# A seven-product scheme for the second matrix product of layer 2, with its weight factors made while layer 1 runs

## The chip, the cores and the metric

The kernel runs on one core of a Trainium2 chip. The metric is the device time of one execution, in microseconds (us). TensorE is called PE here, its weight loads PEld, VectorE DVE, ScalarE ACT, GpSimd POOL, and SyncE, which issues every DMA of this kernel, SP.

## What is computed

Attention in chunks of 64 tokens, then two feed-forward layers on 2304 tokens (width 512, inner width 2048):

```python
x   = chunked_attention(q, k, v)        # 4 x 8 heads x 576 x 64, as 2304 x 512
x2  = mish(x @ w_in1) @ w_out1          # layer 1
out = squareplus(x2 @ w_in2) @ w_out2   # layer 2; squareplus: h if h >= 1, 0 if h <= -1, else (h + 1)^2 / 4
```

The weights come as 64-bit floats, seen as pairs of 32-bit words, and are decoded to 32-bit floats on the chip.

## The kernel before, in words

**Numbers in two parts.** PE multiplies in a rounded 32-bit format (fp32r). To keep precision every operand a is split into hi = round(a) and lo = a - hi, and a product is three matmuls into one accumulator in PSUM: hi hi, hi lo, lo hi. So each operand costs a copy (hi; ACT or DVE) and a subtraction (lo; DVE or POOL), and is twice as large.

**Stages.** Tokens go in 6 blocks of 384 (NB) or 18 tiles of 128; the inner width in 16 row tiles j of 128 or 8 pairs jp.

1. Attention of all tokens, interleaved with the first product of layer 1 (`up`, L569, matmuls at L578): 6 blocks x 16 tiles x 12 matmuls of 384 columns. The activated results z go to DRAM (`z_store`). To about 278 us.
2. The second product of layer 1 (`down` with n = 0, matmuls at L630): per block and j 12 matmuls of 384 columns. `g_pair` (L594) loads a pair of z tiles, copies hi (L273 or L271) and subtracts lo (L608). From 278 us to about 474.
3. The first product of layer 2 (`seven`, L637, matmuls at L654). It uses Strassen's scheme in Winograd's form: a product of 2 x 2 blocks by seven block products in place of eight, at the price of additions. `x_seven` (L406) makes the seven token factors, `w_seven` (L387) the seven weight factors of a pair jp from the decoded weights. 24 units of 42 matmuls of 384 columns. DVE adds up the results (L672) and applies squareplus with ACT (L693, L696, L698). z goes to DRAM again. To about 661 us.
4. The second product of layer 2 (`down` with n = 1, also L630): per block and j, three token tiles by three matmuls of 512 columns, so 6 x 16 x 9 = 864. `g_pair` prepares z as in stage 2; at the end of a block three copies (L786) and three DMAs (L788) write the output. Its weights, split into hi and lo, were put into DRAM in stage 2 (L351) and are fetched by 16 DMAs at the end of stage 3 (`w_back`, L381).

**Weights.** `w_part(n, j)` (L282) decodes one tile of weight n (0 to 3: w_in1, w_out1, w_in2, w_out2): a load of 512 KB, a scaled copy on ACT (L301), a clamp on POOL (L304), three bit operations on DVE (L311, L318, L324), then for n = 2 a store (L344), for the others the split (L329, L333). Before, n = 2 and n = 3 are both decoded in stage 2: tile j of n = 2 is due at t2 + 5 j, of n = 3 at t2 + 82 + 5 j, where t1 is the start of stage 1 in the plan (33 us), t2 that of stage 2 and t3 that of stage 3.

**Order.** A planner (`Plan`, L27) lays every operation on its engine by lengths, due times and releases that stand in the code, and the program is emitted in this order. At run time each engine, and SP's queue, goes through its list strictly in that order.

**Memory.** 154 KB of each partition hold the split operands, at places set by hand (`PLACES`); the rest holds rings of buffers, "ld" (4 of 4 KB), "z2" (6 of 3 KB), "z" (2), "sh" (4) and "dec" (2). PSUM has two groups of four banks, A and B, used in turn.

Of the kernel before, what the change touches and what calls it, by code (L numbers as in the profile page):

```python
# [164 lines left out]
def kernel(  # L165
# [18 lines left out]

    nc = tc.nc
# [41 lines left out]
    for tag, n in PSUM.items():  # L227
# [54 lines left out]
    def w_part(n, j, tau, release=0.0, after=()):  # L282
# [5 lines left out]
        new(sh, "sh", [P, DM])  # L288
# [49 lines left out]
        op("ACT", 0.66, down, reads=[raw], writes=[dec], tiles=[raw, dec], **kw)  # L338
        op("POOL", 0.8, clamp, writes=[dec], tiles=[dec], **kw)
        op("DVE", 0.46, shift, reads=[dec], writes=[sh], tiles=[dec, sh], **kw)  # L340
        op("DVE", 0.69, sign, reads=[dec], writes=[sh], tiles=[dec, sh], **kw)
        op("DVE", 0.72, low, reads=[raw], writes=[sh], tiles=[raw, sh], **kw)
# [38 lines left out]
    def w_back(j, tau, after=()):  # L381
        w = ("wb", j)
        new(w, None, [P, 2, DM], F32R)
        dma(512, lambda _: nc.sync.dma_start(out=get(w).bitcast(F32).rearrange("p r d -> p (r d)"), in_=wd_split[j]),
            reads=[("wd", 3, j), *after], writes=[(w, 0), (w, 1)], tiles=[w], prio=tau)

    def w_seven(n, jp, tau):  # L387


        wf, sf, w = ("wf", n, jp), ("sf", n, jp), ("w7", n, jp)  # L390
        new(sf, "ld", [P, 4, 2 * P])
        new(w, None, [P, 7, 2, 2 * P], F32R)
        A = lambda f, d: lambda: get(wf)[:, f, d * 2 * P:(d + 1) * 2 * P]
# [3 lines left out]
        add(S(1), A(1, 0), A(1, 1), False, reads=[wf], writes=[K(1)], **kw)  # L397
        add(S(3), A(0, 0), A(1, 0), True, reads=[wf], writes=[K(3)], **kw)
        add(S(2), S(1), A(0, 0), True, reads=[wf, K(1)], writes=[K(2)], **kw)
        add(S(4), A(0, 1), S(2), True, reads=[wf, K(2)], writes=[K(4)], **kw)  # L400
        part = lambda a, b: lambda r: get(w)[:, a:b, r]
        split(part(0, 2), lambda: get(wf)[:, 0].rearrange("p (d f) -> p d f", d=2), 4 * P, (w, 0), tau, reads=[wf], tiles=[wf, w])
        split(part(2, 3), lambda: get(wf)[:, 1:2, 2 * P:], 2 * P, (w, 1), tau, reads=[wf], tiles=[wf, w])
        split(part(3, 7), lambda: get(sf), 8 * P, (w, 2), tau, reads=[K(i) for i in (1, 2, 3, 4)], tiles=[sf, w])

    def x_seven(q, tau, after=()):  # L406
# [3 lines left out]
        for d, t in ((0, 0), (0, 1), (1, 1), (1, 0)):  # L410
            x = xs[d, t] = ("xh", q, d, t)
            new(x, "ld", [P, 2, NB])
# [173 lines left out]
    def z_store(n, b, jp, tau):  # L586
        z = ("z", n, b, jp)
        dma(384, lambda _: nc.sync.dma_start(
            out=spill[n][b * NF // 2 + jp], in_=get(z).rearrange("p j t -> p (j t)")
        ), reads=[(z, 0), (z, 1)], writes=[("spill", n, b, jp)], tiles=[z], prio=tau)  # L590

    pairs = {}

    def g_pair(n, b, jp, tau):  # L594

        zl, g = ("zl", n, b, jp), ("g", n, b, jp)
        new(zl, ("z2", "ld")[n], [P, 2, NB])
# [14 lines left out]
    def down(n, b, j, tau):  # L612
        w, g, a = (("w", 1, j), ("wb", j))[n], ("g", n, b, j // 2), j % 2
        ys = [("y", n, b, m) for m in range((KD, TB)[n])]
        if j == 0:
            for y in ys:
                new(y, "AB"[b % 2], [P, 512])

        def products(_):
            wt, gt = get(w), get(g)  # L620
            for m, y in enumerate(ys):
                if n == 0:
                    wh, wl = (wt[:, x, m * P:(m + 1) * P] for x in range(2))
                    gh, gl = gt[:, 0, a], gt[:, 1, a]
                    o, prods = get(y)[:, 0:NB], ((wh, gh), (wh, gl), (wl, gh))
                else:
                    gh, gl = (gt[:, x, a, m * P:(m + 1) * P] for x in range(2))
                    o, prods = get(y), ((gh, wt[:, 0]), (gh, wt[:, 1]), (gl, wt[:, 0]))
                for x, (l, r) in enumerate(prods):
                    nc.tensor.matmul(  # L630
                        out=o, lhsT=l, rhs=r, start=(j == 0 and x == 0), stop=(j == NF - 1 and x == 2)
                    )

        op("PE", 2.09, products, reads=[(g, x) for x in range(2)] + [(w, 0), (w, 1)],
           writes=[*ys, ("step", n, b, j), *([("yend", n, b)] if j == NF - 1 else [])], tiles=[w, g, *ys], prio=tau)
# [100 lines left out]
    for b in range(NBLK):  # L736
        for j in range(NF):
            tau = due2(b, j)
            if j % 2 == 0:
                g_pair(0, b, j // 2, tau - 14)  # L740
            down(0, b, j, tau)
        for m in range(KD):
            y, yo = ("y", 0, b, m), ("yo", b, m)
            new(yo, "sh", [P, NB])
            op(("ACT", "DVE"), (0.49, 0.55), lambda e, yo=yo, y=y: copy(e, get(yo), get(y)[:, 0:NB]),
               reads=[("yend", 0, b)], writes=[yo], tiles=[yo, y], prio=tau)
            dma(192, lambda _, b=b, m=m, yo=yo: nc.sync.dma_start(out=x2d[b][:, m * NB:(m + 1) * NB], in_=get(yo)),
                reads=[yo], writes=[("x2d", b, m)], tiles=[yo], prio=tau)
    t3 = due2(NBLK, 0)
    for bp in range(NBLK // 2):  # L750
        x_seven(bp, (t2 + 80, t3 - 8, t3 + 8)[bp], after=[("step", 0, *((2, 0), (NBLK - 1, 10), (NBLK - 1, NF - 1))[bp])])
    for j in range(NF):
        w_part(2, j, t2 + 5.0 * j, release=t2 + 5.0 * j - 10)
    for j in range(NF):
        w_part(3, j, t2 + 82 + 5.0 * j, release=t2 + 72 + 5.0 * j)
# [8 lines left out]
    for u, (jp, bp) in enumerate(todo):  # L764
        if bp == 0:
# [3 lines left out]
                   after=[("hq", jp - 2, NQ - 1, 0) if jp > 1 else ("step", 0, NBLK - 1, 3 + 5 * jp)])  # L769
# [3 lines left out]
    due4 = lambda b, j: t4 + 2.06 * (b * NF + j)  # L773
    for b in range(NBLK):
        for j in range(NF):
            tau = due4(b, j)
# [6 lines left out]
        for m in range(TB):  # L783
            y, o = ("y", 1, b, m), ("o", b, m)
            new(o, "z", [P, DM])
            op(("ACT", "DVE"), (0.6, 0.69), lambda e, y=y, o=o: copy(e, get(o), get(y)),  # L786
               reads=[("yend", 1, b)], writes=[o], tiles=[y, o], prio=tau)
            dma(256, lambda _, b=b, m=m, o=o: nc.sync.dma_start(  # L788
                out=out[b * NB + m * P:b * NB + (m + 1) * P, :], in_=get(o)
            ), reads=[o], tiles=[o], prio=tau)  # L790
# [54 lines left out]
```

## Time and profile before

| | us |
|---|---|
| runs of the kernel before | 868.79, 868.91, 864.09 (median 868.79) |
| the profiled execution | 863.63 |
| its span, first to last instruction | 861.8 |
| PE busy in the span | 848.0 |
| DVE busy | 548.3 |
| ACT busy | 324.9 |
| POOL busy | 172.5 |

A group of instructions is named by line, engine, operation and shape; its figures are the time in which any of them ran, and the mean length of one in ns. PE's matmuls overlap, so the pace of a stream is not their mean length but the time of a run of them divided by their count. A row of the chain of waits has start, length and what ran. A table by stretch gives busy time and count for each engine, PE's granted clock (1.00 is 2.4 GHz) and the share of time in which the DMA engines moved data.

### The profile page before, as it was taken

What the parts mean: (1) busy time and instruction counts of PE and PEld (TensorE: products, weight loads), DVE (VectorE), ACT (ScalarE), POOL (GpSimd) and SP (SyncE); (2) the same over time, 40 slices, a digit from 0 to 9 for tenths busy, and PEclk for the clock granted to TensorE, in tenths of its full rate; (3) what the DMA queues carried; (4) which work ended last, traced back from release to release, by engine and by line L of the source; (5) the groups of instructions that cost most, each with busy time, mean ns of one, the idle gap of its engine ahead of it and who ended that gap; (6) DMA issues with size and microseconds to landing.
All of it is one profiled execution on the core that took longest, in us unless ns stands there. A gap on an engine that the chain in (4) does not pass through costs nothing.

```text
span 861.8 us, 14614 instructions
## 1 busy us (share of the span) xinstructions
PE 848.0 (98%) x5710; PEld 800.5 (93%) x5710; DVE 548.3 (64%) x875; ACT 324.9 (38%) x535; POOL 172.5 (20%) x154
## 2 busy tenths in 40 slices
PE   9999999999999999999999989999999999999997
PEld 8899999999999999999999989999999888888886
DVE  4998767575402677689888898777776343344331
ACT  3664646565422222224332366666655000000000
POOL 1474212110000201254443463111100000000000
PEclk9999999999999999999999999999999999999999
DMA  8779584867225779759986343333379443443431
GB/s 204 201 217 267 175 225 157 235 184 179 86 110 198 251 255 310 275 168 338 363 306 235 113 152 134 135 135 135 135 266 415 167 130 95 134 138 81 141 108 37
DMA packets 122149, 163.49 MB, mean 190 GB/s; under 512 B 62944, under 2 KB 82400, under 8 KB 122080
## 3 DMA queue, kind: packets, MB, share of 16 engines
q1 hardware_dynamic: 122080, 162.56, 58.5%
q8 instruction: 45, 0.74, 0.4%
q14 instruction: 24, 0.20, 0.1%
HBM read 102.76 MB, written 59.77 MB: 189 GB/s over the span
## 4 chain that ended last, share of the span: by engine, by line
PE 90%; DVE 6%; DMA 1%; issue 1%; ACT 1%; SPq 0%; POOL 0%; DVEq 0%; ACTq 0%; POOLq 0%
PE A L630 23%; PE B L578 21%; PE B L630 20%; PE B L654 10%; PE A L654 10%; PE B L812 2%; PE A L477 2%; PE A L493 1%; DVE memory L311 1%; PE A L549 1%; DVE memory L324 1%; DVE memory L318 1%; PE A L537 1%; DVE memory_r L608 1%; DVE memory_r L273 1%
## 5 line engine op out<-in xcount | busy, mean ns | idle before, releaser
L578 PE MATMUL B<-memory_r 128*128 128x384 f32 x1152 | 213.8, 339 | 1.0 <-POOL memory_r L333 0.8
L630 PE MATMUL B<-memory_r 128*128 128x384 f32 (+1 forms) x1008 | 203.5, 358 | 1.2 <-DVE memory_r L608 0.9
L630 PE MATMUL A<-memory_r 128*128 128x384 f32 (+1 forms) x1008 | 202.1, 358 | 0.4 <-DVE memory_r L608 0.4
L578 PEld LDWEIGHTS B<-memory_r 128*128 128x128 f32 x1152 | 197.6, 188 | 3.6 <-POOL memory_r L333 1.3
L630 PEld LDWEIGHTS B<-memory_r 128*128 128x128 f32 x1008 | 181.1, 188 | 18.8 <-DVE memory_r L608 1.4
L630 PEld LDWEIGHTS A<-memory_r 128*128 128x128 f32 x1008 | 181.1, 188 | 17.5 <-DVE memory_r L608 0.8
L273 DVE CAST memory_r<-memory 128x768 fp32r<-128x768 f32 (+2 forms) x109 | 64.7, 596 | 168.4 <-PE A L630 70.9
L608 DVE TENSOR_TENSOR memory_r<-memory,memory_r 128x768 fp32r<-128x768 f32 x96 | 101.7, 1060 | 18.6 <-ACT memory_r L271 11.3
L304 POOL TENSOR_SCALAR memory<-memory 128x512 f32<-128x512 f32 x64 | 53.3, 835 | 236.6 <-ACT memory L301 216.8
L271 ACT ACTIVATE memory_r<-memory 128x512 fp32r<-128x512 f32 (+3 forms) x80 | 58.4, 745 | 110.7 <-PE A L630 38.8
L654 PE MATMUL B<-memory_r 128*128 128x384 f32 x504 | 92.8, 337 | 3.4 <-DVE memory L672 3.4
L654 PE MATMUL A<-memory_r 128*128 128x384 f32 x504 | 93.2, 335 | 0.1
L654 PEld LDWEIGHTS B<-memory_r 128*128 128x128 f32 x504 | 88.5, 189 | 3.9 <-DVE memory L672 3.7
L654 PEld LDWEIGHTS A<-memory_r 128*128 128x128 f32 x504 | 88.3, 189 | 0.4 <-POOL memory_r L369 0.4
L727 ACT ACTIVATE memory<-B 128x384 f32<-128x384 f32 x96 | 46.0, 491 | 86.9 <-PE B L578 79.9
L271 ACT ACTIVATE memory<-A 128x512 f32<-128x512 f32 (+1 forms) x59 | 32.3, 559 | 114.4 <-PE A L630 64.8
L301 ACT ACTIVATE memory<-memory 128x512 f32<-128x512 f32 x64 | 42.7, 668 | 59.5 <-DMA memory<-in_moe_w_in_dram 34.3
L333 POOL TENSOR_TENSOR memory_r<-memory,memory_r 128x512 fp32r<-128x512 f32 x30 | 43.9, 1465 | 61.7 <-DVE memory_r L273 28.0
L318 DVE SCALAR_TENSOR_TENSOR memory<-memory 128x512 uint32<-128x512 uint32 x64 | 50.5, 793 | 1.2
L324 DVE SCALAR_TENSOR_TENSOR memory<-memory 128x512 uint32<-128x512 uint32 x64 | 49.9, 783 | 1.1
L271 ACT ACTIVATE memory<-B 128x384 f32<-128x384 f32 (+1 forms) x28 | 14.0, 505 | 94.6 <-PE B L630 80.0
L369 POOL TENSOR_TENSOR memory_r<-memory,memory_r 128x768 fp32r<-128x768 f32 (+3 forms) x21 | 40.3, 1923 | 36.7 <-ACT memory_r L271 24.0
(48 smaller groups left out, 644.2 us busy)
## 6 DMA issues: line engine op xcount, KB each, us to landing
z<-memory SPq DMA_DIRECT2D x96, 384.0 KB, 2.6
memory<-z SPq DMA_DIRECT2D x96, 384.0 KB, 4.3
memory<-in_moe_w_in_dram SPq DMA_DIRECT2D x32, 512.0 KB, 5.3
memory<-in_moe_w_out_dram SPq DMA_DIRECT2D x32, 512.0 KB, 5.0
v<-memory_r SPq DMA_DIRECT2D x16, 512.0 KB, 6.4
memory_r<-v SPq DMA_DIRECT2D x16, 512.0 KB, 8.8
memory<-in_v_dram SPq DMA_DIRECT2D x72, 64.0 KB, 3.6
x<-memory SPq DMA_DIRECT2D x24, 192.0 KB, 3.4
```

Of the source, the lines that this page charges most:

```text
L271: nc.scalar.activation(out=out, in_=in_, func=AF.Copy)
L273: nc.vector.tensor_copy(out, in_)
L301: nc.scalar.activation(out=get(dec), in_=get(raw)[:, :, 1].bitcast(F32), func=AF.Copy, scale=DOWN)
L304: nc.gpsimd.tensor_scalar(out=get(dec), in0=get(dec), scalar1=HIGH, scalar2=-HIGH, op0=ALU.min, op1=ALU.max)
L318: nc.vector.scalar_tensor_tensor(out=s, in0=d, scalar=0x80000000, in1=s, op0=ALU.bitwise_and, op1=ALU.bitwise_or)
L324: nc.vector.scalar_tensor_tensor(out=s, in0=get(raw)[:, :, 0], scalar=29, in1=s, op0=ALU.logical_shift_right, op1=ALU.bitwise_or)
L333: eng.tensor_tensor(out=get(w)[:, 1], in0=get(sh), in1=get(w)[:, 0].bitcast(F32), op=ALU.subtract)
L578: nc.tensor.matmul(out=ps, lhsT=a, rhs=xt[:, r, kk, :], start=(kk == 0 and y == 0), stop=(kk == KD - 1 and y == 2),)
L608: op("DVE", 0.98, lambda _: nc.vector.tensor_tensor(out=get(g)[:, 1], in0=get(zl), in1=get(g)[:, 0].bitcast(F32), op=ALU.subtract), reads= ...
L630: nc.tensor.matmul(out=o, lhsT=l, rhs=r, start=(j == 0 and x == 0), stop=(j == NF - 1 and x == 2))
L654: nc.tensor.matmul(out=ps, lhsT=l, rhs=xt[:, r, kk, :], start=(first and kk == 0 and y == 0), stop=(kk == 1 and y == 2), skip_group_check= ...
L727: op("ACT", 0.5, lambda _, h=h, z=z, j=j: nc.scalar.activation(out=get(z)[:, j % 2], in_=get(h)[:, 0:NB], func=AF.Mish), reads=[h], writes ...
```

## The change

Stage 4 gets the seven-product scheme too. The output is made for pairs of token tiles tp (9 of 256 tokens), and each pair of row tiles jp is a 2 x 2 by 2 x 2 block product: seven products of 128 tokens x 128 rows x 256 columns, three matmuls each, into seven half banks of PSUM (four banks). They accumulate over all eight jp before the results are combined once per tp.

- `down_seven` takes the place of `down` for n = 1. For the last jp of a tp it emits the products bank by bank. Then ACT copies one accumulator, seven DVE additions of 256 columns follow and two DMAs of 256 KB write the output.
- `g_seven` takes the place of `g_pair` for n = 1. A unit is one tp and two jp, so 36 units; per unit two DMAs of 256 KB load z (rows of 1 KB; before, rows of 3 KB). DVE does three subtractions for the token factors (512, 256, 256 elements), ACT copies hi (768 and 1024), DVE subtracts lo (768 and 1024). zl and the factors tt take one "ld" buffer each, so two units are in work at a time; the split factors have three buffers. The first two tp are interleaved.
- `w_seven` now serves n = 3 also, in stage 2, with one buffer, and the factors (14 KB a partition for each jp) are stored to DRAM and fetched for stage 4 by `w_back`, two DMAs each way per jp (768 and 1024 KB) in place of one of 512 KB per j.
- w_in2 (n = 2) is decoded from t1 + 115 on, one tile each 9 us: in the second half of stage 1 and not in stage 2. w_out2 (n = 3) is decoded from t2 + 2 on, one pair each 19 us.
- `x_seven` loads the first two token groups into "z2" buffers, where it used "ld" for all. z of layer 2 is stored in another layout (rows of 1.5 KB).

```diff
-    due4 = lambda b, j: t4 + 2.06 * (b * NF + j)
-    for b in range(NBLK):
-        for j in range(NF):
-            if j % 2 == 0:
-                g_pair(1, b, j // 2, tau - 14)
-            if b == 0:
-                w_back(j, tau - 16, after=[("hq", NJ - 1, 0, 0) if j < 6 else (("g", 1, 0, 0), 0)])
-            down(1, b, j, tau)
+    due4 = lambda u: t4 + 5.06 * u
+    units = sorted((unit(tp, jh), tp, jh) for tp in range(NT // (2 * P)) for jh in range(NF // 4))
+    for u, tp, jh in units:
+        g_seven(tp, jh, due4(u) - 30 * (u < 6), due4(u) - 10 - 30 * (u < 6))
+        for jp in {0: (0, 1), 1: (2,), 2: (3,), 3: (4, 5), 4: (6,), 5: (7,)}.get(u, ()):
+            w_back(jp, due4(jp) - 30, False, after=[(("zs", u), 1)])
+    for u, tp, jh in units:
+        for x in range(2):
+            down_seven(tp, 2 * jh + x, due4(u) + 2.53 * x)
...
-        w_part(2, j, t2 + 5.0 * j, release=t2 + 5.0 * j - 10)
-        w_part(3, j, t2 + 82 + 5.0 * j, release=t2 + 72 + 5.0 * j)
+        w_part(2, j, t1 + 125 + 9.0 * j, release=t1 + 115 + 9.0 * j)
+    for jp in range(NF // 2):
+        t = t2 + 2 + 19.0 * jp
+        for j in range(2 * jp, 2 * jp + 2):
+            w_part(3, j, t + 8, release=t, after=[(("sf", 3, jp - 1), 4)] if jp else ())
+        w_seven(3, jp, t + 12)
+        w_back(jp, t + 12, True)
```

The core of the two new functions (in `down_seven`, `SEVEN` lists bank, half, weight factor and token factor):

```python
SEVEN = ((0, 0, 0, 0), (0, 1, 1, 2), (1, 0, 4, 5), (1, 1, 5, 4), (2, 0, 3, 3), (2, 1, 2, 6), (3, 0, 6, 1))
for bank, half, a, c in SEVEN:
    for y, (l, r) in enumerate(((0, 0), (0, 1), (1, 0))):
        nc.tensor.matmul(out=get(ys[bank])[:, half], lhsT=gt[:, l, c], rhs=wt[:, a, r], ...)   # rhs: 256 columns
# g_seven
op("ACT", 0.86, copy(g[:, :, 0, 0:3], zl[:, :, 1:4]))
less(0.7,  tt[:, :, 0:2], zl[:, :, 0:1] broadcast, zl[:, :, 1:3])
less(0.42, tt[:, :, 2], zl[:, :, 2], tt[:, :, 0])
less(0.42, tt[:, :, 3], zl[:, :, 3], tt[:, :, 2])
op("ACT", 1.06, copy(g[:, :, 0, 3:7], tt))
op("DVE", 0.98, g[:, :, 1, 0:3] = zl[:, :, 1:4] - g[:, :, 0, 0:3])
op("DVE", 1.25, g[:, :, 1, 3:7] = tt - g[:, :, 0, 3:7])
```

## Rows read from the trace of the kernel before

**Rows 1.** The page: busy time of each engine over the whole span.

```profile
PE 848.0 (98%) x5710; PEld 800.5 (93%) x5710; DVE 548.3 (64%) x875; ACT 324.9 (38%) x535; POOL 172.5 (20%) x154
```

**Rows 2.** Busy time by stretch (one stage each, the third a transition), all engines.

```profile
37.00:278.00 241.00, 240.02 (x2206) 230.28 (x2205) 148.46 (x289) 126.20 (x208) 53.64 (x52) 1.00 0.63 184
278.00:474.00 196.00, 194.38 (x1117) 193.25 (x1116) 154.65 (x199) 56.57 (x88) 63.60 (x53) 1.00 0.81 278
474.00:520.00 46.00, 42.53 (x235) 41.74 (x235) 41.06 (x52) 23.07 (x39) 25.01 (x14) 0.96 0.38 124
520.00:661.00 141.00, 141.00 (x815) 140.96 (x814) 107.24 (x183) 92.78 (x155) 20.81 (x20) 1.00 0.50 187
661.00:856.00 195.00, 195.00 (x862) 161.49 (x861) 72.44 (x98) 9.67 (x16) 0.00 (x0) 1.00 0.39 124
```

**Rows 3.** Chain of waits: start, length, what; unbroken runs of 384 and 512 columns.

```profile
417.98 27.04 PE A L630 x156
...
697.60 24.48 PE B L630 x108
```

**Rows 4.** Timeline of PE, 28 to 37 us; groups of PEld in the whole trace.

```profile
31.44 1.50 PE L812 MATMUL B<-ident 128*128 128x128 f32 x12
...
L630 PEld LDWEIGHTS B<-memory_r 128*128 128x128 f32 x1008 | 181.1, 188 | 18.8 <-DVE memory_r L608 1.4 <-DVE memory_r L273 0.6
...
L812 PEld LDWEIGHTS B<-ident 128*128 128x128 f32 x166 | 22.3, 212 | 1.8 <-POOL ident masks.py:199 1.4
```

**Rows 5.** Chain of waits at the end of the span.

```profile
856.02 2.05 DMA out_dram<-memory
...
858.17 0.60 ACT memory L271
```

**Rows 6.** Groups of DVE, 662 to 856 us.

```profile
L608 DVE TENSOR_TENSOR memory_r<-memory,memory_r 128x768 fp32r<-128x768 f32 x45 | 43.1, 957 | 7.3 <-ACT memory_r L271 3.3
...
L273 DVE COPY memory<-A 128x512 f32<-128x512 f32 x3 | 2.0, 683 | 0.0
```

**Rows 7.** Groups of DVE and ACT in the whole trace, other sizes.

```profile
L564 DVE TENSOR_TENSOR memory_r<-A,memory_r 128x256 fp32r<-128x256 f32 x36 | 13.3, 410 | 0.1
...
L369 DVE TENSOR_TENSOR memory_r<-memory,memory_r 128x1024 fp32r<-128x1024 f32 x7 | 8.6, 1234 | 3.2 <-ACT memory_r L271 3.2
...
L271 ACT ACTIVATE memory_r<-memory 128x1024 fp32r<-128x1024 f32 x6 | 6.3, 1050 | 0.0
```

**Rows 8.** Groups of DVE, 278 to 474 us.

```profile
L608 DVE TENSOR_TENSOR memory_r<-memory,memory_r 128x768 fp32r<-128x768 f32 x45 | 52.9, 1176 | 8.4 <-ACT memory_r L271 7.9
L318 DVE SCALAR_TENSOR_TENSOR memory<-memory 128x512 uint32<-128x512 uint32 x32 | 25.6, 808 | 0.7
L324 DVE SCALAR_TENSOR_TENSOR memory<-memory 128x512 uint32<-128x512 uint32 x32 | 23.8, 752 | 0.5
L311 DVE TENSOR_SCALAR memory<-memory 128x512 uint32<-128x512 uint32 x32 | 19.2, 609 | 3.8 <-POOL memory L304 2.0 <-POOL memory_r L333 1.2 <-DMA memory<-z 0.5
```

**Rows 9.** DMA issues: whole trace, size each, us to landing.

```profile
memory<-z SPq DMA_DIRECT2D x96, 384.0 KB, 4.3
...
memory<-in_k_dram SPq DMA_DIRECT2D x16, 256.0 KB, 4.6
```

**Rows 10.** All DMA traffic, 632 to 670 us: packets, then issues.

```profile
DMA packets 4616, 14.74 MB, mean 388 GB/s; under 512 B 506, under 2 KB 506, under 8 KB 4614
...
memory_r<-v SPq DMA_DIRECT2D x16, 512.0 KB, 8.8
...
memory<-z SPq DMA_DIRECT2D x8, 384.0 KB, 8.4
```

**Rows 11.** What PE waited for, whole trace (total, times, longest us).

```profile
PE B L654 <- DVE memory L672: 3.4, 1, 3.4
```

**Rows 12.** Busy time by stretch, 158 to 278 us: the first, and their sum.

```profile
158.00:188.00 30.00, 30.00 (x322) 28.88 (x323) 23.04 (x49) 21.68 (x33) 7.02 (x8) 1.00 0.77 219
...
sum 120.00, PE 120.00 PEld 116.78 DVE 51.77 ACT 54.97 POOL 9.30; mean PE 30.00 PEld 29.20 DVE 12.94 ACT 13.74 POOL 2.33
```

More of the change, by code (lines that the diff above doesn't have):

```diff
@@ L379, in add, with w_back @@
            reads=reads, writes=writes, tiles=tiles, prio=tau)
[L381 to L385, printed above, removed]
+    def w_back(jp, tau, store, after=()):
+        w = ("w7s", 3, jp) if store else ("wb", jp)
+        if not store:
+            new(w, None, [P, 7, 2, 2 * P], F32R)
+        for a, b, keys in ((0, 3, (0, 1)), (3, 7, (2,))):
+            here = lambda a=a, b=b: get(w)[:, a:b].bitcast(F32).rearrange("p s r f -> p (s r f)")
+            there = wd_seven[jp][:, a * 4 * P:b * 4 * P]
+            parts = [((w, x), r) for x in keys for r in range(2)]
+            if store:
+                dma(256 * (b - a), lambda _, here=here, there=there: nc.sync.dma_start(out=there, in_=here()),
+                    reads=parts, writes=[("w7d", jp, a)], tiles=[w], prio=tau)
+            else:
+                dma(256 * (b - a), lambda _, here=here, there=there: nc.sync.dma_start(out=here(), in_=there), slow=0.8,
+                    reads=[("w7d", jp, a), *after], writes=parts, tiles=[w], prio=tau)
     def w_seven(n, jp, tau):
-        wf, sf, w = ("wf", n, jp), ("sf", n, jp), ("w7", n, jp)
+        wf, sf, w = ("wf", n, jp), ("sf", n, jp), ("w7" if n == 2 else "w7s", n, jp)
+        wk = [wf] if n == 2 else [(wf, 0), (wf, 1)]
         new(sf, "ld", [P, 4, 2 * P])
         new(w, None, [P, 7, 2, 2 * P], F32R)
-        A = lambda f, d: lambda: get(wf)[:, f, d * 2 * P:(d + 1) * 2 * P]
+        halves = lambda: get(wf).rearrange("p j (d f) -> p j d f", d=2)
+        A = lambda x, y: lambda: halves()[:, x, y] if n == 2 else halves()[:, y, x]
         S = lambda i: lambda: get(sf)[:, i - 1]
@@ L411, in x_seven @@
             x = xs[d, t] = ("xh", q, d, t)
[L412 removed]
+            new(x, "z2" if q < 2 else "ld", [P, 2, NB])
             dma(384, lambda _, x=x, d=d, t=t: nc.sync.dma_start(
@@ L620, in products @@
             wt, gt = get(w), get(g)
+            gh, gl = gt[:, 0, a], gt[:, 1, a]
             for m, y in enumerate(ys):
[L622 to L628, printed above, removed]
@@ new lines, in unit, with g_seven, less @@
+    def unit(tp, jh):
+        return 2 * jh + tp if tp < 2 else tp * (NF // 4) + jh
+    def g_seven(tp, jh, tau, prio):
+        u = unit(tp, jh)
+        zl, tt, g = ("zs", u), ("tt", u), ("g7", u)
+        new(zl, "ld", [P, 2, 4, P])
+        new(tt, "ld", [P, 2, 4, P])
+        new(g, None, [P, 2, 2, 7, P], F32R)
+        blocks = range(2 * tp * P // NB, ((2 * tp + 2) * P - 1) // NB + 1)
+        for x in range(2):
+            jp = 2 * jh + x
+            dma(256, lambda _, x=x, jp=jp: nc.sync.dma_start(
+                out=get(zl)[:, x].rearrange("p (j a) t -> p j (a t)", j=2),
+                in_=spill2[jp].rearrange("p (j t) -> p j t", j=2)[:, :, 2 * tp * P:(2 * tp + 2) * P],
+            ), reads=[*(("spill", 1, b, jp) for b in blocks), *([(("tt", u - 2), 2)] if u > 1 else [])],
+                writes=[(zl, x)], tiles=[zl], prio=prio, release=tau - 24)
+        z, t = [(zl, 0), (zl, 1)], [(tt, x) for x in range(3)]
+        kw = {"prio": prio}
+        def less(length, out, a, b, reads, writes):
+            op("DVE", length, lambda _: nc.vector.tensor_tensor(out=out(), in0=a(), in1=b(), op=ALU.subtract),
+               reads=reads, writes=writes, tiles=[zl, tt], **kw)
+        op("ACT", 0.86, lambda _: copy("ACT", get(g)[:, :, 0, 0:3], get(zl)[:, :, 1:4]),
+           reads=z, writes=[(g, 0)], tiles=[zl, g], **kw)
+        less(0.7, lambda: get(tt)[:, :, 0:2], lambda: get(zl)[:, :, 0:1].to_broadcast([P, 2, 2, P]),
+             lambda: get(zl)[:, :, 1:3], z, t[:1])
+        less(0.42, lambda: get(tt)[:, :, 2], lambda: get(zl)[:, :, 2], lambda: get(tt)[:, :, 0], [*z, t[0]], t[1:2])
+        less(0.42, lambda: get(tt)[:, :, 3], lambda: get(zl)[:, :, 3], lambda: get(tt)[:, :, 2], [*z, t[1]], t[2:])
+        op("ACT", 1.06, lambda _: copy("ACT", get(g)[:, :, 0, 3:7], get(tt)), reads=t, writes=[(g, 1)], tiles=[tt, g], **kw)
+        for length, a, b, x, c, keys, y in (
+            (0.98, 0, 3, zl, 1, z, 0),
+            (1.25, 3, 7, tt, 0, t, 1),
+        ):
+            op("DVE", length, lambda _, a=a, b=b, x=x, c=c: nc.vector.tensor_tensor(
+                out=get(g)[:, :, 1, a:b], in0=get(x)[:, :, c:], in1=get(g)[:, :, 0, a:b].bitcast(F32), op=ALU.subtract
+            ), reads=[*keys, (g, y)], writes=[(g, 2 + y)], tiles=[x, g], **kw)
@@ new lines, with down_seven, emit, plus @@
+    SEVEN = ((0, 0, 0, 0), (0, 1, 1, 2), (1, 0, 4, 5), (1, 1, 5, 4), (2, 0, 3, 3), (2, 1, 2, 6), (3, 0, 6, 1))
+    def down_seven(tp, jp, tau):
+        u = unit(tp, jp // 2)
+        g, w = ("g7", u), ("wb", jp)
+        ys = [("y7", tp, i) for i in range(4)]
+        if jp == 0:
+            for y in ys:
+                new(y, "AB"[tp % 2], [P, 2, 2 * P])
+        def emit(banks):
+            for bank, half, a, c in SEVEN:
+                if bank not in banks:
+                    continue
+                wt, gt = get(w), get(g)[:, jp % 2]
+                for y, (l, r) in enumerate(((0, 0), (0, 1), (1, 0))):
+                    nc.tensor.matmul(
+                        out=get(ys[bank])[:, half], lhsT=gt[:, l, c], rhs=wt[:, a, r],
+                        start=(jp == 0 and half == 0 and y == 0), stop=(jp == NF // 2 - 1 and y == 2),
+                        skip_group_check=True,
+                    )
+        for banks in ((0,), (1,), (2,), (3,)) if jp == NF // 2 - 1 else (range(4),):
+            n = sum(x[0] in banks for x in SEVEN)
+            op("PE", 0.361 * n, lambda _, banks=banks: emit(banks),
+               reads=[(g, x) for x in range(4)] + [((w, x), r) for x in range(3) for r in range(2)],
+               writes=[ys[i] for i in banks], tiles=[w, g, *(ys[i] for i in banks)], prio=tau)
+        if jp < NF // 2 - 1:
+            return
+        pu, u2, u3 = (("e7", tp, i) for i in range(3))
+        o = [("o", tp, i) for i in range(2)]
+        for t, tag in ((pu, "dec"), (u2, "sh"), (u3, "sh")):
+            new(t, tag, [P, 2 * P])
+        for t in o:
+            new(t, "z", [P, 2, 2 * P])
+        kw = {"prio": tau - EARLY}
+        def plus(bank, half, b, out, writes, tiles):
+            op("DVE", 0.42, lambda _: nc.vector.tensor_tensor(
+                out=out(), in0=get(ys[bank])[:, half], in1=get(b), op=ALU.add
+            ), reads=[ys[bank], b], writes=writes, tiles=[ys[bank], b, *tiles], **kw)
+        op("ACT", 0.42, lambda _: copy("ACT", get(pu), get(ys[0])[:, 0]), reads=[ys[0]], writes=[pu], tiles=[ys[0], pu], **kw)
+        plus(0, 1, pu, lambda: get(o[1])[:, 0], [(o[1], 0)], [o[1]])
+        plus(1, 0, pu, lambda: get(u2), [u2], [u2])
+        plus(1, 1, u2, lambda: get(u3), [u3], [u3])
+        plus(2, 0, u2, lambda: get(u2), [u2], [])
+        plus(2, 0, u3, lambda: get(o[0])[:, 1], [(o[0], 1)], [o[0]])
+        plus(2, 1, u3, lambda: get(o[1])[:, 1], [(o[1], 1)], [o[1]])
+        plus(3, 0, u2, lambda: get(o[0])[:, 0], [(o[0], 0)], [o[0]])
+        for i in (1, 0):
+            t = 2 * tp + i
+            dma(256, lambda _, i=i, t=t: nc.sync.dma_start(
+                out=out[t * P:(t + 1) * P, :], in_=get(o[i]).rearrange("p d f -> p (d f)")
+            ), reads=[(o[i], 0), (o[i], 1)], tiles=[o[i]], prio=tau)
@@ L772 @@
     t4 = t3 + 7.31 * len(todo)
-    due4 = lambda b, j: t4 + 2.06 * (b * NF + j)
-    for b in range(NBLK):
-        for j in range(NF):
-            tau = due4(b, j)
-            if j % 2 == 0:
-                g_pair(1, b, j // 2, tau - 14)
-            if b == 0:
-                w_back(j, tau - 16, after=[("hq", NJ - 1, 0, 0) if j < 6 else (("g", 1, 0, 0), 0)])
-            down(1, b, j, tau)
[L783 to L790, printed above, removed]
+    due4 = lambda u: t4 + 5.06 * u
[5 more added lines that the diff above has]
+    for u, tp, jh in units:
+        for x in range(2):
+            down_seven(tp, 2 * jh + x, due4(u) + 2.53 * x)
     idle = ("idle",)
```

104 lines of the change are left out of this document (59 added, 45 removed).

## The prediction

> **What bounds the kernel now.** I read the engine totals first: PE is busy 848.0 of 861.8 us, DVE only 548.3 [rows 1]. The table by stretch shows that this holds in every stage: PE runs without a gap from 520 to 856 us, and is short by 1.6 us in stage 2 and by 3.5 in the transition from 474 to 520, where its granted clock also drops (0.96) [rows 2]. So the time is PE's instruction stream, and what shortens that stream is gained as long as PE stays fed. DVE is nearest to becoming the bound in stage 2 (154.7 of 196) and in the transition (41.1 of 46); in stage 4 it is busy only 72.4 of 195 [rows 2]. The only long wait of PE that remains is 3.4 us in the transition, for DVE [rows 11].
>
> The execution that all this comes from took 863.6 us; the three runs have a median of 868.8, 5.2 higher, with one at 864.1. I make the sum against 863.6 and place the result between these two levels at the end.
>
> **PE in stage 4: the main term.** Before, 864 matmuls of 512 columns. Their pace in an unbroken run is 24.48 / 108 = 226.7 ns; the pace at 384 columns is 27.04 / 156 = 173.3 ns [rows 3]. 128 columns more cost 53.3 ns, so a matmul costs 13.3 ns and 0.417 ns a column, and one of 256 columns should take 120.0 ns. After, 9 tp x 8 jp x 7 products x 3 = 1512 matmuls. So 864 x 0.2267 = 195.8 us become 1512 x 0.1200 = 181.4: **-14.4 us**. The scheme saves 12.5% of the columns (442,368 to 387,072, 23.0 us) and gives 8.6 us back as the fixed part of 648 more matmuls.
>
> No matmul of 256 columns in this format is in the trace, so the pace is bounded by neighbours. Each matmul loads its own 128 x 128 weights, and the record of such a load is 188 ns [rows 4], longer than 120. It does not follow that loads limit the pace: the fillers of L812 have loads of 212 ns on the mean, and 12 of them run in 1.50 us [rows 4]. The merged piece includes the last matmul's whole length, so its pace is at most 1.50 / 12 = 125 ns. Loads that long do follow each other faster than they last. The low end is the columns alone, 256 x 0.417 = 107 ns (161 us, -34.5 in all); the high end is 188, one whole load record each (284 us, +88.5). I take 120, on the line through the two paces of the same kind of matmul; the filler piece lies near it, and neither end does.
>
> The Trainium skill has a rule that speaks against this: "TensorE: Matmul & The Clock Gate", in "What overlaps and what doesn't" of "The mechanism", says that a weight load overlaps a running matmul only when they use different row groups, and here every load and matmul uses all rows. The trace disagrees: at 512 columns 226.7 ns hold 213 ns of columns at 2.4 GHz, and 13 ns would be left for the load. The same page gives a load 107 ns for 128 columns ("LDWEIGHTS (loading the stationary operand)"); hidden behind 120 ns of matmul by that figure, but not with much to spare.
>
> **Feeding stage 4: DVE and ACT.** Per unit DVE does one operation of 512 elements (683 ns, from the row of that size), two of 256 (410 each), one of 768 (957) and one of 1024 (1234) [rows 6, 7]: 3.69 us. Per tp that is four units and seven additions of 256: 14.8 + 2.9 = 17.6 us, against 8 x 21 x 0.120 = 20.16 us of PE. DVE goes from 37% to 87% busy, and 2.5 us per tp are left. ACT does at most 2 x 1.05 per unit [rows 7], under half its time. I take this as hidden: **0**. The best case is 0 as well, since PE sets the pace. If the cover goes, DVE sets it: at the price of 1176 ns that the 768-element subtraction has in stage 2, where POOL works too, against 957 in stage 4 [rows 6, 8], everything is 1.23 times as long, 21.7 us per tp, and 9 x 1.5 = 13.8 us go. POOL has nothing to do in stage 4, so I take the stage-4 price.
>
> The loads: two units are in work at a time. A new z load can go out when the older unit's zl is read, about 2.5 us after its data landed (0.68 + 0.41 + 0.41 + 0.96). A z load of 384 KB lands in 4.3 us, one of 256 KB in far smaller pieces in 4.6 [rows 9]. With two issues the loop is 2.5 + 4.6 + 1 = 8 us for two units, against 10.1 us of PE.
>
> **The start of stage 4.** The weight factors are 8 x 14 KB x 128 = 14.7 MB in place of 8.4. From 632 to 670 us the DMA engines moved 14.74 MB at 388 GB/s, weights and z together, and z loads took 8.4 us in it instead of 4.3 [rows 9, 10]. With 6.3 MB more the burst lasts 21.0 / 0.388 = 54 us, to about 686. The last factor is used by unit 6, at 661 + 6.5 x 5.04 = 694. There are 8 us of margin, and the plan loads each factor after the z of an earlier unit, so z is not behind all of it: **0**. If the margin is overrun, PE waits at units 4 to 6, and I price that at the burst's whole addition less the margin, up to 8 us.
>
> **Layer 1.** PE's work there does not change. In stage 2 DVE loses 16 decodes of 808 + 752 + 609 = 2.17 us, 34.7 us [rows 8], and the splitting of w_out2. It gains eight `w_seven`: four additions of 256, subtractions of 512, 256 and 1024: 8 x (4 x 0.41 + 0.68 + 0.41 + 1.23) = 31.7 us if POOL takes none. So stage 2 is no fuller than before. The 34.7 us land between 158 and 290 us, where DVE is busy 51.8 of 120 us, though 23.0 of the first 30 [rows 12]; that first part is crowded, and the plan's due times let the decode give way to the tail of 278. SP issues 32 loads and stores there that it used to issue in stage 2; behind one that waits stand attention's loads, which are due about a block of 42 us ahead. The stores of the factors wait for the last split on SP's queue, with layer 1's z loads behind them; three split buffers (12 us of PE) cover that, as they covered the 16 stores before. **0**; ends: the wait of 3.4 us in the transition with its slow clock, about 4.5 together, may go or may come a second time.
>
> **The tail.** Before, the last output copy had to wait for an earlier output DMA (2.05 us) and started at 858.17 [rows 5]. After, two buffers suffice for two outputs; the last of the seven additions ends about 1.7 us after the last matmul (they queue on DVE, banks being finished 0.7 us apart) and the DMA follows. I make it **-0.4**, within -1.6 and +0.8.
>
> **Sum.** -14.4 - 0.4 = -14.8: 863.6 becomes 848.8 for an execution like the profiled one, 854.0 for one like the median. I predict the middle, **851.4**; my own range for this case is 844 to 858.
>
> **Rivals.**
> - *Part of the gain goes into new waits* (the start of stage 4, or stage 2 where `x_seven` now takes four of six "z2" buffers from the z loads). For it: DVE at 79% in stage 2 and DMA at its limit from 632 us [rows 2, 10]. Against: PE lost only 1.6 us in stage 2 with as much DVE work. Price: 8 us at the start of stage 4 and 4.5 in layer 1, so 848.8 + 12.5 = 861, 863 between the levels.
> - *DVE sets the pace of stage 4, and the kernel is slower.* The place is `g_seven`: within a unit DVE needs ACT's copy of the factors before its last subtraction, and landing z before its first. With b us of waiting per unit the stage takes 9 x (17.6 + 4 b). It leaves PE's pace at b = 0.63 and equals the old stage at b = 1.04; from there it is slower. At b = 1.5 it is 212 us, +17, about 883. For it: 87% busy leaves little. Against: DVE lost 7.3 us before 45 subtractions in stage 4, 0.16 each [rows 6], and order within a unit puts the other subtraction beside ACT's copy.
> - *Weight loads do not hide at 256 columns.* At 188 ns the stage takes 284 us: 940. From 129.5 ns on (195.8 / 1512) nothing is gained. For it: the load's record [rows 4] and the rule above, by which the time would be near this. Against: the fillers' pace.
>
> **Chances.** The forecast 0.70, lost to waits 0.17, DVE-bound 0.10, loads 0.03. The range from 843 to 867 takes in the loss of 4.5 us kept or gained, the waits, and the near half of the DVE case; about 0.15 are outside. A difference under 1% (8.7 us) is about what a measurement of this kernel cannot tell from none. Faster by more than that, below 860.1: the forecast and a fifth of the waits, 0.73. Within 1%: the other waits and a third of the DVE case, 0.17. Slower: the rest, 0.10.
>
> **What would show it.** In the changed profile: matmuls of 256 columns 120 ns apart; the stretch of stage 4 about 181 us with PE busy throughout and DVE near 87%; PE's row of waits without `g_seven`'s lines; DVE in stage 2 at or under 155 us, and some 80 of 120 in the second half of stage 1; DMA near 390 GB/s for over 50 us around the start of stage 4. Wrong would be: PE waiting for DVE once per unit in stage 4, a pace over 125 ns, or a wait at units 4 to 6 for a factor's DMA.

## The result and the profile after

The changed kernel took 853.08 us (median of four runs, 852.36 to 853.55) against 867.64 for the kernel before (four runs, 864.09 to 868.91): a ratio of 0.984, 95% interval 0.981 to 0.987. Measured again in a later set beside eight runs of the kernel before (median 864.5) the ratio was 0.989, 0.986 to 0.992. Single executions of that set that ran in a much slower state (1164 to 1700 us) are left out, here and below. So the changed kernel is 1.1 to 1.6% faster, some 9 to 15 us; 851.4 was predicted.

The profiled execution of the changed kernel took 853.2 us, 10.4 less than the profiled one of before. From the first and last matmul of each stage:

| | before | after | difference |
|---|---|---|---|
| start of stage 2 | 278.1 | 278.7 | +0.6 |
| stages 2 and 3 | 382.6 | 386.4 | +3.8 |
| stage 4 | 195.9 | 181.4 | -14.5 |
| last matmul to the end | 5.4 | 5.1 | -0.4 |

(After, the first 21 matmuls of stage 4 run before the end of stage 3; their 2.5 us are counted in stage 4. Stage 4 is counted with the pace of its last matmul; the last row begins at that matmul's start, so the two overlap by 0.1 to 0.2 us.)

The table by stretch of the changed kernel, the same stretches as in [rows 2]:

```profile
37.00:278.00 241.00, 239.14 (x2199) 229.25 (x2198) 168.46 (x320) 135.40 (x226) 70.59 (x71) 1.00 0.76 227
278.00:474.00 196.00, 193.14 (x1105) 192.66 (x1104) 143.77 (x189) 54.44 (x82) 58.75 (x47) 0.99 0.74 259
474.00:520.00 46.00, 42.16 (x232) 40.90 (x232) 42.51 (x52) 21.61 (x35) 22.93 (x12) 0.97 0.34 115
520.00:661.00 141.00, 140.60 (x808) 140.28 (x808) 111.05 (x189) 91.57 (x154) 29.36 (x23) 1.00 0.51 180
661.00:856.00 195.00, 185.69 (x1537) 185.49 (x1535) 143.99 (x242) 71.28 (x86) 0.00 (x0) 0.99 0.48 166
```

DVE's load moved as the change says: up by 20 us in stage 1, down by 11 in stage 2 (154.7 before), and doubled in stage 4 (72.4 before). PE has lost time in stage 2 and in the transition, where it waited for DVE; this is its table of waits (total, times, longest), to be held against [rows 11]:

```profile
PE A L777 <- DVE memory_r L381: 3.4, 2, 2.8
PE B L650 <- DVE memory_r L633: 2.9, 1, 2.9
```

L650 and L777 are the old L630 and L654, L633 the old L608, L381 and L388 the old L369 and L376. No wait for stage 4's preparation (L682, L696) is in that table. The chain of waits of the changed kernel at two places, the run of 256-column matmuls in stage 4 and the end of the wait near 514 us:

```profile
514.79 2.49 DVE memory_r L381
517.28 0.04 issue
517.33 4.79 PE A L777 x17
...
768.58 15.12 PE B L720 x126
```

The last row is the main term: 15.12 / 126 = 120.0 ns, as read off the two paces of [rows 3]. The row at 517.33 shows what a wait of 3 us costs on top: 17 matmuls in 4.79 us, 282 ns each in place of 173, since the granted clock fell to 0.50 (1.2 GHz) half a us after the wait of 3 us had ended, and by their starts ten of them ran at 320 ns. From 522 us on it was 1.00 again. The row by stretch just after the wait:

```profile
518.00:520.00 2.00, 2.00 (x8) 2.00 (x7) 1.91 (x5) 0.00 (x0) 2.00 (x2) 0.50 0.42 166
```

### The profile page after: what moved, and what is told of

It is laid out like the page before. It is cut to its first block, busy times and chain, and to the rows that moved or that the text cites. A ratio compares the mean times of both kernels' runs of the same rounds, so it can differ in the third digit from the quotient of the medians.

```text
span 851.5 us, 16231 instructions
## 1 busy us (share of the span) xinstructions
PE 835.2 (98%) x6358; PEld 821.2 (96%) x6358; DVE 634.1 (74%) x1043; ACT 390.8 (46%) x612; POOL 191.3 (22%) x167
## 5 line engine op out<-in xcount | busy, mean ns | idle before, releaser
L275 ACT ACTIVATE memory_r<-memory 128x768 fp32r<-128x768 f32 (+3 forms) x160 | 129.7, 838 | 203.1 <-DVE memory L388 33.5
L603 PE MATMUL B<-memory_r 128*128 128x384 f32 x1152 | 213.6, 339 | 1.0 <-POOL memory_r L345 0.8
L650 PE MATMUL B<-memory_r 128*128 128x384 f32 x576 | 105.1, 338 | 2.9 <-DVE memory_r L633 2.9
L650 PEld LDWEIGHTS B<-memory_r 128*128 128x128 f32 x576 | 101.4, 190 | 3.3 <-DVE memory_r L633 3.2
L720 PE MATMUL A<-memory_r 128*128 128x256 f32 x840 | 103.5, 283 | 0.0
L650 PE MATMUL A<-memory_r 128*128 128x384 f32 x576 | 102.0, 334 | 0.0
L650 PEld LDWEIGHTS A<-memory_r 128*128 128x128 f32 x576 | 100.2, 188 | 0.0
L777 PE MATMUL A<-memory_r 128*128 128x384 f32 x504 | 94.8, 339 | 3.8 <-DVE memory_r L381 3.4
L777 PEld LDWEIGHTS A<-memory_r 128*128 128x128 f32 x504 | 89.3, 191 | 4.7 <-DVE memory_r L381 4.0
L777 PE MATMUL B<-memory_r 128*128 128x384 f32 x504 | 91.6, 335 | 0.5 <-DVE memory L795 0.4
L696 DVE TENSOR_TENSOR memory_r<-memory,memory_r 128x768 fp32r<-128x768 f32 (+1 forms) x72 | 77.2, 1088 | 16.4 <-ACT memory_r L275 15.7
L777 PEld LDWEIGHTS B<-memory_r 128*128 128x128 f32 x504 | 87.6, 188 | 1.1 <-DVE memory L795 1.1
L720 PE MATMUL B<-memory_r 128*128 128x256 f32 x672 | 83.1, 283 | 0.0
L381 POOL TENSOR_TENSOR memory_r<-memory,memory_r 128x512 fp32r<-128x512 f32 (+3 forms) x33 | 62.3, 1892 | 73.8 <-ACT memory_r L275 46.2
L277 DVE CAST memory_r<-memory 128x768 fp32r<-128x768 f32 (+3 forms) x61 | 39.2, 642 | 35.5 <-PE B L650 19.3
L633 DVE TENSOR_TENSOR memory_r<-memory,memory_r 128x768 fp32r<-128x768 f32 x48 | 53.2, 1111 | 13.8 <-ACT memory_r L275 9.4
L275 ACT ACTIVATE memory<-A 128x512 f32<-128x512 f32 (+2 forms) x59 | 31.2, 540 | 66.6 <-PE A L502 21.1
```

The source lines that it names most:

```text
L275: nc.scalar.activation(out=out, in_=in_, func=AF.Copy)
L277: nc.vector.tensor_copy(out, in_)
L381: eng.tensor_tensor(out=out(1), in0=in_(), in1=out(0).bitcast(F32), op=ALU.subtract)
L603: nc.tensor.matmul(out=ps, lhsT=a, rhs=xt[:, r, kk, :], start=(kk == 0 and y == 0), stop=(kk == KD - 1 and y == 2),)
L633: op("DVE", 0.98, lambda _: nc.vector.tensor_tensor(out=get(g)[:, 1], in0=get(zl), in1=get(g)[:, 0].bitcast(F32), op=ALU.subtract), reads= ...
L650: nc.tensor.matmul(out=get(y)[:, 0:NB], lhsT=l, rhs=r, start=(j == 0 and x == 0), stop=(j == NF - 1 and x == 2))
```

## The experiments

**How far fewer columns pay.** In the kernel before, each matmul of stage 4 is cut along its columns, into two and into four:

```diff
-                    nc.tensor.matmul(out=o, lhsT=l, rhs=r, ...)
+                    cut = 2 if n else 1          # 4 in the second kernel
+                    c = r.shape[-1] // cut
+                    for s in range(cut):
+                        nc.tensor.matmul(out=o[:, s * c:(s + 1) * c], lhsT=l, rhs=r[:, s * c:(s + 1) * c], ...)
```

> The kernel before, each of the 864 matmuls of 512 columns in stage 4 cut into two of 256 with the same weights (1728, each with its own load); nothing else changes. Theory (a matmul costs 13.3 ns and 0.417 ns a column, weight loads hidden): 1728 x 0.120 = 207.4 us in place of 195.8, so stage 4 is 11.5 us longer, at a pace of 120 ns. Rival (the load's record of 188 ns limits the pace): 1728 x 0.188 = 324.9, 129 us longer.

> The same cut into four of 128 columns (3456 matmuls), to find how far weight loads stay hidden. Theory of the line alone: 13.3 + 53.3 = 66.7 ns, 230.4 us, stage 4 34.6 us longer. Rival, a floor set by the weight load near 107 to 112 ns (what the Trainium skill gives a load of 128 columns, in TensorE: Matmul & The Clock Gate, LDWEIGHTS, and near the pace of the 128-column fillers): 370 to 387 us, 174 to 191 us longer. I lean to the floor.

They took 872.5 and 1052.6 us, beside 864.9 for the kernel before (one execution each; in that of the halves stage 4 began 2.4 us sooner than in the profiled one of before). A run of matmuls in the chain of waits of each, halves first (L633 is the old L630 in both):

```profile
731.86 25.92 PE A L633 x216
```

```profile
733.46 48.24 PE B L633 x432
```

That is 120.0 ns at 256 columns, on the line, and stage 4 lasts 207.4 us: 11.5 longer, as worked out. At 128 columns it is 111.7 ns and not 66.7; stage 4 lasts 386. So there is a floor. That loading 128 x 128 weights for each matmul sets it is argued and not shown: no run has these matmuls without their loads. The Trainium skill gives such a load 107 ns ("TensorE: Matmul & The Clock Gate", "LDWEIGHTS (loading the stationary operand)"), and the measured floor is close to it. Its rule that a load overlaps a matmul only in other row groups ("The mechanism" of the same page) does not hold here: by that figure 111.7 ns contain both the load and 53 ns of columns. The floor and the line meet at (111.7 - 13.3) / 0.417 = 236 columns, an estimate, since no width between 128 and 256 was run; by it the change stopped just above the width at which nothing more is to be had.

**How much room DVE has in stage 4.** In the changed kernel one operation is done twice in every unit, a token-factor subtraction of 256 elements, or the lo subtraction of 1024:

```diff
+        less(0.42, tt[:, :, 3], zl[:, :, 3], tt[:, :, 2])
...
             (1.25, 3, 7, tt, 0, t, 1),
+            (1.25, 3, 7, tt, 0, t, 1),
```

> The changed kernel with the last token-factor subtraction (256 elements, 0.42 us) done twice in each of the 36 units, so DVE's work per tp in stage 4 is 17.7 + 1.7 = 19.4 us beside PE's 20.16. Theory A (DVE's idle time in stage 4 is slack only, about 2.5 us per tp): hidden, stage 4 stays within 2 us. Theory B (DVE's waits for ACT and z, 0.7 us per unit in the changed kernel's trace, are part of each unit's chain and stay): 9 x (19.4 + 2.7) = 199 us, 17 us longer.

> The changed kernel with the last lo subtraction (1024 elements, 1.22 us) done twice in each unit: DVE's work per tp is 17.7 + 4.9 = 22.6 us, over PE's 20.16. Theory A (DVE sets the pace with hardly any waits): 9 x 22.6 = 203 us, stage 4 about 22 us longer. Theory B (waits of 0.7 us per unit stay): 9 x 25.3 = 228, about 46 longer. If the stage does not grow, DVE's work per unit was misread.

With 0.42 us more the time was 856.2 and stage 4 182.8 us, 1.4 longer: hidden, so DVE's waits for ACT were slack. With 1.22 more it was 866.0, and stage 4 194.4, 13 longer and not 22. Busy times after stage 3 of the changed kernel, then of the run with 1.22 more, as a whole and from 726 us on:

```profile
668.00:846.00 178.00, 178.00 (x1486) 178.00 (x1485) 137.40 (x228) 67.90 (x80) 0.00 (x0) 1.00 0.48 164
```

```profile
669.00:859.00 190.00, 182.81 (x1476) 181.23 (x1475) 172.10 (x261) 68.19 (x80) 0.00 (x0) 0.97 0.45 149
726.00:859.00 133.00, 132.97 (x1106) 132.53 (x1105) 125.80 (x192) 47.46 (x55) 0.00 (x0) 1.00 0.37 117
```

All of PE's waits in that stage (7.2 us, with slow clock after them) lie before 726 us. From there on PE runs at full pace, while DVE is busy 89.2 of the 90 us from 756 to 846. So DVE keeps up with PE even so, and neither theory is right: both price DVE by the lengths of its records, and these overlap. Two of them, one after the other:

```profile
757.52 1.22 DVE L697 TENSOR_TENSOR memory_r<-memory,memory_r 128x1024 fp32r<-128x1024 f32 x1
758.66 0.42 DVE L743 TENSOR_TENSOR memory<-B,memory 128x256 f32<-128x256 f32 x1
```

The second starts 1.14 us after the first, not 1.22. From start to start the subtractions take 0.60 (512), 0.34 (256), 0.87 (768) and 1.14 us (1024), each some 0.08 less than its record. A tp is then 4 x 3.28 + 7 x 0.33 = 15.4 us of DVE in the changed kernel, and 20.0 with the 1024 twice: just under PE's 20.16, and not 22.6. What costs the 13 us is the start of the stage; why the longer units lose there was not followed.

**Whether the sooner decode of w_in2 matters, and when stage 4's preparation must begin.** A control changes only how early the first six units are due; the second kernel decodes w_in2 later as well.

```diff
-        g_seven(tp, jh, due4(u) - 30 * (u < 6), due4(u) - 10 - 30 * (u < 6))
+        g_seven(tp, jh, due4(u) - 15 * (u < 6), due4(u) - 10 - 15 * (u < 6))
...
-        w_part(2, j, t1 + 125 + 9.0 * j, release=t1 + 115 + 9.0 * j)
+        w_part(2, j, t2 - 20 + 9.0 * j, release=t2 - 30 + 9.0 * j)      # second kernel only
```

> The changed kernel with the preparation of the first six units of stage 4 due 15 us ahead of their use in place of 30. A control for the next runs, whose order of work needs this. Theory: the buffers come free later than the due time anyway, so no difference: within 2 us of 853. Rival: z of the first units comes later, behind more of the weight factors, and PE waits at units 0 to 3: 2 to 8 us more.

> The control with w_in2 decoded later again: tile j from t2 - 30 + 9 j on, so about 11 of its 16 tiles in stage 2 in place of 2 or 3. DVE gets some 8 x 2.2 = 18 us more between 278 and 400 us. Theory (DVE in stage 2 has 52 us idle in the changed kernel's trace, and PE's one wait there is a crowding at one spot, so the sooner decode brings little by itself): within 3 us of the control. Rival (the sooner decode is what makes the change possible): DVE above 90% in stage 2, PE waits more, 5 us or more over the control.

The control took 857.4 us (ratio to before 0.991, 0.988 to 0.994), the later decode 855.5 (0.988, 0.984 to 0.992). By their times the control and the changed kernel (0.984 and 0.989) cannot be told apart for certain; the traces can. In the control PE waits five times between 687 and 708 us, as the rival says, and stage 4 lasts 186.6, in the slowest of its five executions. With the later decode and the same lead it lasts 182.8, so the cost of the shorter lead varies. What DVE waited for in the control, 668 to 712 us:

```profile
DVE memory L682 <- DMA memory<-zz: 8.0, 4, 3.9
```

z is late: between 632 and 690 us, where weight factors are loaded too, a z load lands in 10.7 us on the median in the control, in 8.4 in the changed kernel and in 6.0 with the later decode. The first rival of the prediction had named this place. In the changed kernel, with 30 us of lead, PE does not wait. The decode, by contrast, does not matter: stages 2 and 3 take 386.4 us in the control and 386.3 with the later decode, though DVE is busy 165.8 us of 196 in stage 2 in place of 143.2.

**What PE's waits come from.** In the changed kernel DVE has much idle time in stage 2 and PE waits all the same. The timelines of DVE and of POOL around the wait at 374 us show why:

```profile
368.00 3.16 DVE L388 TENSOR_TENSOR memory<-memory 128x768 f32<-128x768 f32 x1
371.08 0.55 DVE L277 CAST memory_r<-memory 128x768 fp32r<-128x768 f32 x1
371.55 0.94 DVE L388 TENSOR_TENSOR memory<-memory 128x768 f32<-128x768 f32 x1
372.42 2.60 DVE L381 TENSOR_TENSOR memory_r<-memory,memory_r 128x768 fp32r<-128x768 f32 x1
374.95 2.55 DVE L633 TENSOR_TENSOR memory_r<-memory,memory_r 128x768 fp32r<-128x768 f32 x1
```

```profile
367.32 3.02 POOL L381 TENSOR_TENSOR memory_r<-memory,memory_r 128x1024 fp32r<-128x1024 f32 x1 [2.25 <-DVE memory_r L277]
371.70 4.98 POOL L381 TENSOR_TENSOR memory_r<-memory,memory_r 128x768 fp32r<-128x768 f32 x2 [1.36 <-DVE memory_r L277]
```

An addition or subtraction of 768 elements takes 0.94 us or 2.5 to 3.2, and the long ones end just after an instruction of POOL's does: the first 0.82 us after POOL's at 367.32, the last 0.82 us after the pair at 371.70. Four kernels take POOL's additions and subtractions away: all of them with 15 us of lead, those of 768 elements only, all of them with 20 us of lead, and all of them in the kernel before.

```diff
-        op(("DVE", "POOL"), (0.15 + width / 930, 0.15 + width / 370), lo, ...)      # split, L381
+        op("DVE", 0.15 + width / 930, lo, ...)
...
-        op(("DVE", "POOL"), (0.15 + width / 930, 0.15 + width / 370), emit, ...)    # add, L388
+        op("DVE", 0.15 + width / 930, emit, ...)
```

> The control with all subtractions and additions of x_seven and w_seven (lines 381 and 388) on DVE; POOL keeps the clamps and the splits of w_in1 and w_out1. In the changed kernel 63 of them run on POOL after 278 us, 95 us of POOL. On DVE they would take 44 us at undisturbed lengths; but DVE instructions beside them are 41 us longer than their undisturbed lengths, so theory A: DVE's busy time stays within 8 us, and as each result comes sooner the waits of PE at 374 and 514 us (2.9 and 3.4 us, and the slow clock after each) shrink: 3 to 9 us faster than the control. Theory B (POOL's help is real, its overlap with longer DVE instructions a coincidence): DVE's busy time grows by 30 us or more after 278 us, and PE waits more: 3 us or more slower.

> The control with only the operations of 768 elements (those of x_seven) taken from POOL to DVE; the smaller ones of w_seven may still go to POOL. Theory A as for the run before: these 16 are the ones beside PE's two waits, so 2 to 8 us faster than the control. Theory B: DVE is the fuller for it and the waits get longer, 2 us or more slower.

> The changed kernel with the operations of lines 381 and 388 on DVE alone and the first six units of stage 4 due 20 us ahead in place of 30 or 15. Theory: taking POOL out removes some 8 us of PE's waits and slow clock in stages 2 and 3, and with 20 us of lead the z loads go out ahead of more of the weight factors, so that the 5.5 us that the 15 us lead cost between 677 and 695 us go too: 843 to 848, 5 to 10 us under the changed kernel. Rival (the waits at the start of stage 4 come from the slower units with DVE alone, not from the lead): 849 to 851, waits of PE for line 696 near 680 us stay.

> The kernel before with its additions and subtractions of lines 369 and 376 on DVE alone, POOL keeping the clamps and the splits of line 333. Theory: the gain of taking POOL out is independent of the seven-product scheme in stage 4; PE's wait of 3.4 us at 512 us and the slow clock after it go, 3 to 7 us faster than before. Rival: in this kernel DVE also decodes w_in2 in stage 2, so DVE gets too full and nothing is gained.

| | time, us | ratio to before | stages 2 and 3 | stage 4 |
|---|---|---|---|---|
| control, lead 15 | 857.4 | 0.991 (0.988 to 0.994) | 386.4 | 186.6 |
| only those of 768 on DVE, lead 15 | 853.0 | 0.986 (0.981 to 0.990) | 380.3 | 184.9 |
| all on DVE, lead 15 | 849.6 | 0.982 (0.979 to 0.985) | 376.8 | 187.1 |
| all on DVE, lead 20 | 847.9 | 0.980 (0.979 to 0.982) | 376.8 | 184.3 |
| kernel before, all on DVE | 861.3 | 0.997 (0.996 to 0.998) | 380.2 | 195.9 |

The times are medians, the stages those of the profiled executions (860.1, 855.2, 850.7, 848.9 and 860.5 us). Theory A holds. Busy times of the whole execution, the control and the one with everything on DVE and the same lead, and their rows by stretch:

```profile
PE 837.6 (98%) x6358; PEld 822.3 (96%) x6358; DVE 634.0 (74%) x1044; ACT 391.1 (46%) x612; POOL 188.8 (22%) x166
278.00:668.00 390.00, 382.94 (x2189) 380.87 (x2188) 300.89 (x435) 170.57 (x277) 108.48 (x80) 0.99 0.60 211
```

```profile
PE 833.4 (98%) x6358; PEld 819.4 (97%) x6358; DVE 619.8 (73%) x1084; ACT 405.2 (48%) x634; POOL 94.1 (11%) x104
278.00:668.00 390.00, 388.71 (x2267) 387.53 (x2266) 295.21 (x488) 190.61 (x306) 14.68 (x18) 1.00 0.62 222
```

62 operations came to DVE from POOL, and the planner handed 22 copies from DVE to ACT. DVE runs 40 instructions more and is busy 14 us less. At undisturbed lengths what came is 43 us and what went 11, so the rest of DVE's instructions lost over 40 us, an estimate. The copies are a second change in this run, not tried apart; the last run below hands ACT more of them and gains nothing. Stages 2 and 3 take 9.6 us less, 2.4 over what 2160 matmuls at 173.3 ns need. Of DVE's long instructions beside POOL's the Trainium skill says the same, in "SBUF — State Buffer", "Who interferes with whom": VectorE and GpSimd share a pair of ports to SBUF, an instruction of VectorE with two inputs there meets one of GpSimd that reads there, and the second is blocked until the first ends. The trace agrees, with 0.95 us become 2.5 to 3.2.

In the kernel before the same edit brings 0.3%, at the lower edge of what was expected, and 2.4 us of stages 2 and 3. Its split of w_out2 (L333) stays on POOL there, and POOL is still busy 37.7 of 196 us in stage 2. With 20 us of lead in the changed kernel, the waits at the start of stage 4 do not go: stage 4 is still 2.9 us longer than with 30. It is faster than both kernels: in one set its executions took 846.3 to 848.9 us, those of the changed kernel 852.1 to 856.7.

> The changed kernel once more, beside the next runs on one chip: 852 to 856, 1.0 to 2.0% under the kernel before.

It was 0.989 (0.986 to 0.992) of the kernel before, which is what the result above gives; its time lies where expected, the gain at the lower edge.

A last run takes the hi copies of layer 1's z from DVE in the kernel with 20 us of lead:

```diff
-        op(("ACT", "DVE"), (0.86, 0.57), lambda e: copy(e, get(g)[:, 0], get(zl)),
+        op("ACT", 0.86, lambda e: copy(e, get(g)[:, 0], get(zl)),
```

> The run before, with the hi copies of layer 1's z pairs on ACT alone (they were shared with DVE). DVE loses some 25 copies of 0.56 us in stage 2, ACT is under a third busy there. Theory: PE's last wait in stage 2 (1.3 us near 380 us) goes, 0 to 3 us faster. Rival: ACT's copy takes 0.85 us for 0.56 and a pair gets ready later, so the same or 1 to 3 us slower.

Its ratio was 0.983 (0.981 to 0.985), no better and perhaps 2 us worse. The wait near 380 us shrank as expected, from 1.3 to 0.25 us; but another of 3.0 us came at 523, with the slow clock behind it. Why was not followed.

## Why the prediction was right, and where it was off

- **PE in stage 4, -14.4.** Right, by its own step: 120.0 ns a matmul and 181.4 us (-14.5 as measured). The bounds were 107 and 188; the choice of the line through two paces of the same kind of matmul held, and the cut into halves shows it by itself.
- **Feeding stage 4, 0.** Right: PE never waits for `g_seven`. DVE was expected 87% busy; between 668 and 846 us it is 137.4 of 178, 77%. The price was too high: 17.6 us per tp adds up record lengths, which overlap by 0.08 us each; from start to start it is 15.4, 77% of 20.16. The run with 0.42 us more per unit shows that the cover is real, the one with 1.22 more that it lasts to 99% once the start of the stage is over.
- **The start of stage 4, 0.** Right, with less to spare than I gave it. Between 632 and 690 us the changed kernel moved 21.68 MB at 374 GB/s, 58 us, where 54 were expected. PE did not wait, but in the four runs with 15 us of lead for 30 stage 4 is 1.4 to 5.7 us longer.
- **Layer 1, 0 within 4.5 either way.** This is the term that was off: +3.8. DVE's load in stage 2 did fall (143.8 from 154.7), and I took that for safety. But what PE waited for was DVE's few instructions that stand behind POOL's, and a mean load says nothing of these. The row that showed it was in the text: the 768-element subtraction at 1176 ns in stage 2 and 957 in stage 4 [rows 6, 8]. I read it as a price of 1.23 and not as six instructions of 2.0 to 2.6 us and six of 1.2 to 1.4 among 33 of 0.95. That `x_seven` now takes buffers from the z loads may have a part in the wait at 374 us. This was not tried by itself; with everything on DVE `x_seven` takes them too, and a wait of 1.1 us at 380 us is left.
- **The tail, -0.4.** Right: 5.43 to 5.05 us after the last matmul's start.
- **The rivals.** Loads that limit the pace: false at 256 columns; at 128 there is a floor, whatever sets it. Its price of 940 was added up wrongly: 88.5 us are counted from the old stage, so from 851.4 it is 284 - 181.4 more, about 954. DVE setting the pace: not here, with 0.42 us per unit free from the start on and 1.22 later. New waits: partly true, 3.8 us of the 12.5 priced.
- **The level.** The profiled execution of before was a low one of its four runs, so the sum against it, 848.8, missed by 4.4, and the sum against the median, 854.0, by 0.9; the middle lay between. That 851.4 came within 1.7 us is in part luck: the 2.6 us added for the level made up for most of the 3.8 lost in layer 1, and the sum of -14.8 stands against -10.4 between the two profiles. In the later set the kernel before was at 864.5, and the gain nearer to the profile's 10.4 than to 14.6.

## What to carry to other kernels

Before a product is cut into more and narrower matmuls, fit a pace per column and per matmul from two widths in the trace, and look for the floor: here 13.3 ns + 0.417 ns a column, and 112 ns at 128 columns. Price a chain of DVE instructions from start to start, not by record lengths: here 15.4 us in place of 17.6. Work handed to POOL to relieve DVE is to be priced by what DVE's instructions beside it lose, in a histogram of lengths and not in a mean; here 95 us of POOL's work cost DVE about as much as doing it, over 40 us. The first loads of a new stage want to be issued before the bulk load of that stage and not merely in time on paper: here a shorter lead cost 1.4 to 5.7 us.

## What was not expected of the hardware

A matmul with its own weights has a floor of 111.7 ns (128 columns), so going from 256 columns to 128 saves 7%. Taking 62 operations onto DVE, with 22 copies going to ACT, lowered its busy time by 14 us. And a wait of PE of 3 us costs about 4.5: ten matmuls after it run at 320 ns in place of 173.
